# A token and channel mixer on one core: channel products in groups of six feature blocks, two places for token products in each chunk

## The chip, the cores and the metric

The kernel runs on one core of one Trainium2 chip. The metric is the time of one execution in microseconds (us). The engines are named as the profile names them: PE is TensorE (PEld its weight loads), DVE is VectorE, ACT is ScalarE, POOL is GpSimd, SP is SyncE, which here only issues transfers.

## What is computed

Of a batch of 8 sequences with 4096 tokens and 192 features, the kernel computes a softmax-weighted sum over seven earlier tokens (eight heads of 24 features), and feeds it to a mixer with two pairs of products. The mixer's four weight matrices are float64, and the kernel converts them.

```python
w = softmax(weight_gen, over the 7 taps)
x = sum over k of w[:, :, head, k] * x_pad[:, s + k]        # (8, 4096, 192)
h = relu(x.T @ w_tok1) @ w_tok2                             # tokens: 4096 -> 256 -> 4096
u = x + h.T
out = u + relu(u @ w_ch1) @ w_ch2                           # channels: 192 -> 1536 -> 192
```

Products keep nearly full float32 precision: each operand is split in a high and a low part, and a product is three matmuls (high by high, high by low, low by high).

## The kernel before

A sequence is cut into eight chunks of 512 tokens, 64 chunks in all; chunk g belongs to sequence g // 8. Five kinds of work meet on PE:

- **First token product** (T1, `token1`, L497, L499, for the first two sequences L514): one chunk of the weighted sums against `w_tok1`, accumulated over the eight chunks of a sequence in `h1s`. All eight must be there before the sequence's second token products can start (`make_h1`).
- **Second token product** (T2, `token2`, L531): 10 matmuls that give u of one chunk.
- **First channel product** (C1, `channel1`). The 1536 hidden features are 12 blocks of 128, taken as six pairs. The 192 input features are 128 plus 64: for the 128 (`a_hi`, `a_lo`) a pair takes 6 matmuls on all 128 rows of the array (L574); for the other 64 (`c_hi`, `c_lo`) the two blocks of a pair use the two halves of the rows at once, 6 matmuls in 3 steps of two (L579). Within a group of pairs all L574 come first, then all L579.
- **Second channel product** (C2, `channel2`, L595): 10 matmuls on 128 rows for each pair, accumulated in `acc`.
- In the first 120 us, the weighted sums and T1 of the first sequence, and conversions of weights.

Before the change a group is two pairs: 24 matmuls of C1, 20 of C2, three groups to a chunk, 192 groups in all. C2 of a group follows C1 of the next group, so PE alternates C1, C2, C1, C2; after a C2 there is a place for one token product, T1 or T2 (`pick`).

Results of C1, T1 and T2 land in PSUM, in three places of two banks (`ps_w`, taken in turn); `acc` has the other two banks. From a place of C1 (`ph`), ACT writes the high part of relu (L582) and DVE the low part (L583) into a tile `h`, of which there are four. T1 and T2 start from a value that ACT copies into their place first (L490, L525); T1 of a sequence's first chunk from zeros that DVE writes (`memset`, L487). After T2, ACT and DVE move u to the single tile `uf` (L538 to L543), and `u_parts` splits it into `a_hi`, `a_lo`, `c_hi`, `c_lo` (two tiles of each, L550 to L555). `acc` of a chunk is set from `uf` by ACT (`seed`, L603), after DVE has taken the chunk before out of it (`store`, L612, L613); ACT then moves the result to `out_tile` in 12 pieces (L622).

DVE's other large work is the weighted sums of later chunks (`attention`, L214, L228; POOL adds part of them by DMA, L232), up to twelve chunks ahead. Weights of `w_tok2` are converted from float64 chunk by chunk in the first 250 us (`convert`: three ACT steps L155 to L157, three DVE steps L159 to L161, then `split`, L166, L167), and those of `w_tok1` come back from DRAM for each later T1 (`load_w1`, `val<-s`, L379, or `w<-s`, L390).

The order on each engine is fixed when the program is built. A planner (`pump`) keeps a clock for each engine (`at`), with cost constants (`C1`, `C2`, `T1` and others), and fills ACT and DVE with pieces of the chains (`attentions`, `turns`, conversions, `store`, `u_parts`) up to a limit that depends on when the next `h` is due (`next_lo`, `SLACK`). On the chip each engine works through its list in order and waits where an operand or a place is not ready.

Of the kernel before, what the change touches and what calls it, by code (L numbers as in the profile page):

```python
# [21 lines left out]
def mixer_kernel(ctx: ExitStack, tc: tile.TileContext, x, wg, wt1, wt2, wc1, wc2, out):  # L22
# [13 lines left out]
    NQ = NP // 2  # L36
# [226 lines left out]
    def two_parts(m):  # L263
# [9 lines left out]
        if m // NCH >= F1:  # L273
            yield "a", 860, hi
            yield "v", 880, lo
# [205 lines left out]
    def token1(m):  # L481
# [4 lines left out]
        if i == 0:  # L486
            nc.vector.memset(th[:, :, cols], 0.0)  # L487
            h1s[b] = late.tile([P, KR, 2 * D], F32, tag="h1s", name="h1s")[:, :, cols]
        else:
            nc.scalar.copy(th[:, :, cols], h1s[b])  # L490
        yield
        if b >= F1:
            xh = xht.pop(m)
            for r in range(KR):
                for c in range(CT):
                    rs = slice(r * P, (r + 1) * P)
                    nc.tensor.matmul(th[:, r, 0:2 * D], w[:, c, 0, rs], xh[:, c, :], start=False, stop=False,  # L497
# [3 lines left out]
        else:  # L501
            token1_float(th, w, m, None, CT - 1)
# [16 lines left out]
    def token2(m, up=None):  # L519
# [25 lines left out]
    def u_parts(m):  # L545
# [3 lines left out]
        a_hi, a_lo, c_hi, c_lo = (late.tile([P, N], F32R, tag=x, name=x, bufs=2) for x in ("a_hi", "a_lo", "c_hi", "c_lo"))  # L549
# [15 lines left out]
    def channel1(g, q):  # L565

        a_hi, a_lo, c_hi, c_lo = ut[g]
        pairs = [2 * q, 2 * q + 1]
# [11 lines left out]
        for p in pairs:  # L580
            h = ht[g, p] = late.tile([P, 2, 2, N], F32R, tag="h", name="h", bufs=4)
# [5 lines left out]
    def channel2(g, q):  # L587
        acc = acc_t[g]
        for p in (2 * q, 2 * q + 1):
# [66 lines left out]
    LAST = 690  # L656
    T1, T1F, T2 = 2264, 2600, 2270
    TOP, LOW = 1000, 1180
    h_at, w_at, h1_at, h1s_at = {}, deque([0.0] * 3), {0: 0.0}, [0.0]
    free = {"acc": 0.0, "u": 0.0, "t": 0.0}  # L660
    pr_free = deque([0.0] * PR)
    xa_at, soft_at, wg_at, stored_at = {}, {}, {}, {}
# [40 lines left out]
    def pump(limit, keys=()):  # L703

        scalar = 0
        while True:
            best = None
            now = max(at["act"], at["pe"])
            end = max(at["pe"], w_at[0], w_at[1]) + C1 - LAST + LATE
# [34 lines left out]

    def next_lo():

        return max(at["act"], max(at["pe"], w_at[0], w_at[1]) + C1 - LAST + HOP) + TOP + HOP

# [5 lines left out]
             "done": NCH - 1, "w1": NCH}  # L754

    def raw_free(tag):

        if state["jobs"]:
            job, *what = state["jobs"].popleft()
            fetch_w2(*what, tag) if job is convert_w2 else fetch_channel(*what, tag)  # L760
            add_chain(job(*what), max(at["pe"], at["dve"]) + LOAD if at["pe"] > 0 else SOON, (job, *what))
# [47 lines left out]
    with tc.tile_pool(name="pro", bufs=1) as pro, \  # L809
# [30 lines left out]
        for m in range(NCH):  # L840
# [43 lines left out]
        state["jobs"] = deque((convert_w2, i) for i in range(1, NCH))  # L884
# [16 lines left out]
    load_xt(2)  # L901
    run(last)
    at["dve"], at["act"] = 3500, 1500
    chains[0:0] = [Chain(attentions()), Chain(turns()), Chain(soft)]
    add_chain(convert_channel("c2", 2), 0.0, ("c2", 2))
# [3 lines left out]
    def begin_token1():  # L909
        m, t = ready.popleft()  # L910
        it = token1(m)
        next(it)
        return it, m, on("act", 480 if m < F1 * NCH else 900, t, w_at.popleft(), h1s_at[0])

    def do_token1(it, m, t):
# [3 lines left out]
        pump(end + SLACK_M)  # L919
# [5 lines left out]
        while state["w1"] < min(m + 1 + (m + 1 >= F1 * NCH), NG - 1):  # L925
# [8 lines left out]
    def do_token2(it, m, t):  # L934
        next(it)
        t = on("pe", T2, t, h1_at[m // NCH])
        pump(t + SLACK_M)
        next(it, None)
        t = on("dve", 690, on("act", 1250, t))
# [8 lines left out]
    def token1_ready(soon=100):  # L948
        return ready and ready[0][0] in w1t and ready[0][1] <= at["pe"] + soon
# [5 lines left out]
    def pick(g, q, soon):  # L955
        final = (g + 1) % NCH == 0 and (g + 1) // NCH not in h1t and g + 1 < NG
        first = token1_ready(soon)
        if first and (final or q != 1 and ready[0][0] <= g + NCH + 2):
            return do_token1, begin_token1()
        if token2_ready(g + 1, soon):  # L960
            return do_token2, begin_token2(g + 1)
        if first and ready[0][0] <= g + NCH + 2:
            return do_token1, begin_token1()

    seed(0)
    for g in range(NG + 1):
        for q in range(NQ if g < NG else 1):
            if g == 0 and q > 0:
                need(lambda: ("w1a", 1) in done)
            if g == 1 and q == 0:  # L970
                need(lambda: ("c2", 2) in done, ("c2", 2))
            picked = None
            if g < NG:
                channel1(g, q)
                end = on("pe", C1, w_at.popleft(), w_at.popleft(), free["u"] if q == 0 else 0.0)
                for t in (end - LAST, end):
                    h_at[g, q] = on("dve", LOW, on("act", TOP, t))
                    w_at.append(h_at[g, q])
                picked = pick(g, q, C2)
            n = g * NQ + q - 1  # L980
            if n >= 0:
                prev = divmod(n, NQ)
                channel2(*prev)
# [11 lines left out]
            pump(next_lo() + (SLACK if g > NCH else SLACK0))  # L995
            if g == NG:
                break
            picked = picked or pick(g, q, 100)
            if picked is None:
                continue  # L1000
            picked[0](*picked[1])
            pump(next_lo() + SLACK)
        if state["token2"] < g + 1 < NG:
            while (g + 1) // NCH not in h1t:
                need(token1_ready, ("w1", state["token1"] + 1), ("x", state["token1"] + 1))
                do_token1(*begin_token1())
            need(lambda: g + 1 in w2t and g + 1 in xbt, (convert_w2, g + 1))
            do_token2(*begin_token2(g + 1))
        need(lambda: g + 1 in ut or g + 1 >= NG, ("u", g + 1))
# [29 lines left out]
```

## Time and profile before

| | before |
|---|---|
| median of 3 runs | 2193.71 us (2193.71 to 2195.42) |
| the profiled execution | 2193.25 us, its span 2191.5 us |
| PE busy | 98% of the span |
| DVE, ACT busy | 71%, 58% |

The span runs from the first to the last instruction; 1.8 us of the execution lie around it. Busy time of PE says little of its pace, since matmuls overlap: a matmul of 512 columns is shown 390 to 400 ns long, while one starts every 227 ns. So PE is read by the starts of its matmuls: the distance from one to the next is what the step costs.

### The profile page before, as it was taken

The numbers are of one execution on the slowest core, as the hardware profiler recorded it, in microseconds if no ns is written. First come the engines' busy times: TensorE is split into PE (matmuls) and PEld (weight loads), VectorE is DVE, ScalarE is ACT, GpSimd is POOL, SyncE is SP. The second block draws the span as 40 slices with busy tenths as digits, with TensorE's granted clock in tenths as the row PEclk, the third lists the DMA queues.
The fourth block names the chain that finished last, engine by engine and source line by source line (L and its number), as shares of the span: only waits on it lengthen the run. The fifth ranks groups of instructions, "written<-read, shape, count | busy, mean of one in ns | idle before, by whom it ended". The sixth has DMA issues, their size and how long they took to land.

```text
span 2191.5 us, 27185 instructions
## 1 busy us (share of the span) xinstructions
PE 2139.4 (98%) x10438; PEld 1671.6 (76%) x10438; DVE 1545.9 (71%) x1756; ACT 1264.6 (58%) x1972; POOL 164.8 (8%) x202
## 2 busy tenths in 40 slices
PE   7989999799999999999999999999999999999998
PEld 5757777677777877777777777777777777777776
DVE  8987887688888868777776876867787764333333
ACT  5557665456655655556565555556555565555554
POOL 0000111001110010000000010000100000000000
PEclk9999999899999999999999999999999999999999
DMA  7665778768778866755675665666667563222210
GB/s 274 216 222 156 196 203 192 205 179 241 206 209 248 225 178 174 195 139 175 174 200 167 182 164 153 189 170 189 176 176 195 139 169 96 68 68 68 64 34 18
DMA packets 165826, 366.66 MB, mean 167 GB/s; under 512 B 16456, under 2 KB 104264, under 8 KB 150336
## 3 DMA queue, kind: packets, MB, share of 16 engines
q1 hardware_dynamic: 138304, 285.74, 41.8%
q0 software_dynamic: 26496, 77.61, 18.3%
q8 instruction: 82, 1.34, 0.2%
q10 hardware_dynamic: 896, 1.57, 0.2%
q14 instruction: 48, 0.39, 0.1%
HBM read 225.13 MB, written 70.52 MB: 135 GB/s over the span
## 4 chain that ended last, share of the span: by engine, by line
PE 91%; DMA 3%; DVE 2%; ACT 2%; issue 1%; SPq 1%; POOL 0%; ACTq 0%; POOLq 0%; DVEq 0%
PE acc L595 39%; PE ph L574 23%; PE ph L579 13%; PE up L531 6%; PE tapsum L340 3%; PE th L497 3%; PE th L514 2%; PE th L499 2%; ACT out_tile L622 1%; DMA xb<-xs 1%; DMA xt<-in_x_dram 1%; PE turn L350 0%; DMA xs<-t 0%; ACT h L582 0%; DMA s<-w 0%
## 5 line engine op out<-in xcount | busy, mean ns | idle before, releaser
L595 PE MATMUL acc<-h,w2s 128*128 128x512 f32 x3840 | 926.3, 395 | 0.0
L595 PEld LDWEIGHTS acc<-h,w2s 128*128 128x128 f32 x3840 | 706.1, 188 | 208.2 <-issue 59.8
L583 DVE SCALAR_TENSOR_TENSOR h<-ph,h 128x1024 fp32r<-128x1024 f32 x384 | 451.7, 1218 | 328.9 <-ACT h L582 327.0
L582 ACT ACTIVATE h<-ph 128x1024 fp32r<-128x1024 f32 x384 | 373.2, 1025 | 366.0 <-PE ph L579 365.2
L214 DVE TENSOR_TENSOR pr<-xt,wn 128x768 f32<-128x768 f32 x336 | 312.0, 949 | 7.0 <-DMA xa<-pr 6.7
L574 PE MATMUL ph<-a_hi,w1a_hi 128*128 128x512 f32 x768 | 303.3, 395 | 9.3 <-ACT a_hi L550 7.4
L574 PE MATMUL ph<-a_lo,w1a_hi 128*128 128x512 f32 x768 | 301.0, 392 | 1.7 <-DVE a_lo L552 1.6
L574 PE MATMUL ph<-a_hi,w1a_lo 128*128 128x512 f32 x768 | 300.9, 392 | 0.0
L232 POOL DMA_DIRECT2D xa<-pr x176 | 151.2, 859 | 1447.4 <-DVE pr L228 1167.2
L603 ACT COPY acc<-uf 128x1024 f32<-128x1024 f32 x64 | 65.1, 1017 | 262.2 <-DVE oc L613 262.2
L622 ACT COPY out_tile<-oa 32x256 f32<-32x256 f32 x512 | 206.7, 404 | 6.8
L574 PEld LDWEIGHTS ph<-a_hi,w1a_hi 128*128 128x128 f32 x768 | 145.2, 189 | 39.6 <-ACT a_hi L550 8.9
L579 PE MATMUL ph<-c_hi,w1c_hi 64*128 64x512 f32 x768 | 171.6, 444 | 0.0
L574 PEld LDWEIGHTS ph<-a_lo,w1a_hi 128*128 128x128 f32 x768 | 145.2, 189 | 34.1 <-DVE a_lo L552 3.7
L574 PEld LDWEIGHTS ph<-a_hi,w1a_lo 128*128 128x128 f32 x768 | 145.4, 189 | 28.3
L531 PE MATMUL up<-w,h 128*128 128x512 f32 x630 | 156.8, 396 | 5.5 <-ACT up L525 5.4
L228 DVE TENSOR_TENSOR pr<-pr 128x768 f32<-128x768 f32 x160 | 152.7, 954 | 4.0
L579 PE MATMUL ph<-c_lo,w1c_hi 64*128 64x512 f32 x768 | 151.6, 391 | 0.0
L579 PE MATMUL ph<-c_hi,w1c_lo 64*128 64x512 f32 x768 | 150.8, 389 | 0.0
L531 PEld LDWEIGHTS up<-w,h 128*128 128x128 f32 x630 | 119.7, 191 | 32.5 <-ACT up L525 7.2
L579 PEld LDWEIGHTS ph<-c_hi,w1c_hi 64*128 64x128 f32 x768 | 71.7, 183 | 77.4 <-issue 66.5
L543 DVE TENSOR_TENSOR uf<-up,uf 64x512 f32<-64x512 f32 x63 | 42.9, 681 | 109.1 <-ACT uf L539 109.1
(83 smaller groups left out, 2054.1 us busy)
## 6 DMA issues: line engine op xcount, KB each, us to landing
w<-s SPq DMA_DIRECT2D x96, 1024.0 KB
xa<-pr POOLq DMA_DIRECT2D x176, 384.0 KB, 5.4
xt<-in_x_dram SPq DMA_DIRECT2D x56, 960.0 KB
out_dram<-out_tile SPq DMA_DIRECT2D x128, 192.0 KB
xs<-t SPq DMA_DIRECT2D x58, 384.0 KB
xb<-xs SPq DMA_DIRECT2D x348, 64.0 KB
raw<-in_moe_w_tok_dram SPq DMA_DIRECT2D x16, 1024.0 KB
s<-w POOLq DMA_DIRECT2D x8, 1024.0 KB, 6.9
```

Of the source, the lines that this page charges most:

```text
L214: nc.vector.tensor_mul(t.rearrange("p t (h g) -> p (t h) g", h=H).rearrange("p (o n) g -> p o n g", o=1), x_k, w)
L228: nc.vector.tensor_add(sums[m], sums[m], prt.pop(m))
L232: nc.gpsimd.dma_start(xat[m].rearrange("p t d -> p (t d)"), sums[m].rearrange("p t d -> p (t d)"), accum_op=ALU.add)
L340: nc.tensor.matmul(ps[:, n, 0:half * D], ident, prs[k][:, n * half:(n + 1) * half, :], start=k == 0, stop=k == K - 1)
L497: nc.tensor.matmul(th[:, r, 0:2 * D], w[:, c, 0, rs], xh[:, c, :], start=False, stop=False, skip_group_check=True)
L531: nc.tensor.matmul(up[:, n, :], h1[:, k, d], w[:, l, k * N:(k + 1) * N], start=k == 0 and j == 0 and not seeded, stop=k == KR - 1 and j == ...
L574: nc.tensor.matmul(ph[p][:, j, :], w[:, fs], u, start=n == 0, stop=False)
L579: nc.tensor.matmul(ph[p][:, j, :], w[rows, p * P:(p + 1) * P], u[rows], start=False, stop=n == 2)
L582: nc.scalar.activation(h[:, :, 0, :], ph[p], AF.Relu)
L583: nc.vector.scalar_tensor_tensor(h[:, :, 1, :], ph[p], 0.0, h[:, :, 0, :].bitcast(F32), op0=ALU.max, op1=ALU.subtract)
L595: nc.tensor.matmul(acc[:, n, :], w2s[:, f, d], h[:, j, l, :], start=False, stop=f == NF - 1 and i == len(steps) - 1, skip_group_check=True)
L622: nc.scalar.copy(dst, src[to:to + Q].rearrange("p (n e d) -> p n e d", n=2, d=Q)[:, n])
```

## The change

Six things change in the program. A group is three pairs (six feature blocks) instead of two, so there are two groups to a chunk, 128 in all, and a group takes all three PSUM places. `h` has five tiles; for that, `a_hi`, `a_lo`, `c_hi` and `c_lo` have one tile each, and `u_parts` of a chunk waits until the last C1 of the chunk before is done. At each of the two places of a chunk T2, T1 or both can stand (`picks`). T1 of a first chunk needs no zeros: its first matmul overwrites. The second chunk's `w_tok2` weights are fetched and converted before the last third of `w_ch2`. T1's weights are fetched two ahead from the fourteenth chunk on, and the planner's constants and limits are other ones.

```diff
-    NQ = NP // 2
+    PQ = 3
+    NQ = NP // PQ
@@ two_parts, load_w1
+            yield "w", 0, lambda: free["xh"]
...
+            w1_at[m] = at["pe"] + FETCH
@@ token1
-            nc.vector.memset(th[:, :, cols], 0.0)
...
-                    nc.tensor.matmul(th[:, r, 0:2 * D], w[:, c, 0, rs], xh[:, c, :], start=False, stop=False,
+                    nc.tensor.matmul(th[:, r, 0:2 * D], w[:, c, 0, rs], xh[:, c, :], start=i + c == 0, stop=False,
...
-            token1_float(th, w, m, None, CT - 1)
+            token1_float(th, w, m, 0 if i == 0 else None, CT - 1)
@@ token2
+            nc.scalar.copy(u[c, 1, :], up[e, 1, :])
             nc.scalar.copy(u[:, 0, :], up[:, 0, :])
-            nc.scalar.copy(u[c, 1, :], up[e, 1, :])
@@ u_parts
-        a_hi, a_lo, c_hi, c_lo = (late.tile([P, N], F32R, tag=x, name=x, bufs=2) for x in ("a_hi", "a_lo", "c_hi", "c_lo"))
+        a_hi, a_lo, c_hi, c_lo = (late.tile([P, N], F32R, tag=x, name=x) for x in ("a_hi", "a_lo", "c_hi", "c_lo"))
+        yield "gate", 0, lambda: state["channel1"] >= m * NQ
+        yield "w", 0, lambda: free["parts"]
@@ channel1, channel2
-        pairs = [2 * q, 2 * q + 1]
+        pairs = range(PQ * q, PQ * (q + 1))
...
-            h = ht[g, p] = late.tile([P, 2, 2, N], F32R, tag="h", name="h", bufs=4)
+            h = ht[g, p] = late.tile([P, 2, 2, N], F32R, tag="h", name="h", bufs=5)
...
-        for p in (2 * q, 2 * q + 1):
+        for p in range(PQ * q, PQ * (q + 1)):
@@ the planner's constants
+    FETCH = 6000
-    SOON = 500
-    SLACK = 900
-    SLACK0 = 1000
+    SOON = 5500
+    SLACK = 2500
-    LATE = 300
-    C1, C2 = 4390, 4540
+    LATE = 1500
+    C1, C2 = 6570, 6820
@@ the weights of the second chunk
-                fetch_channel("c2", 2)
+                fetch_w2(1)
...
-        state["jobs"] = deque((convert_w2, i) for i in range(1, NCH))
+        state["jobs"] = deque([(convert_channel, "c2", 2)] + [(convert_w2, i) for i in range(2, NCH)])
@@ do_token1
-        while state["w1"] < min(m + 1 + (m + 1 >= F1 * NCH), NG - 1):
+        while state["w1"] < min(m + 1 + (m >= F1 * NCH - 3), NG - 1):
@@ the token products of a place
-    def pick(g, q, soon):
...
+    def picks(g, soon):
+
+        two = token2_ready(g + 1, soon)
+        if two:
+            yield do_token2, begin_token2(g + 1)
+        if token1_ready(soon) and ready[0][0] <= g + NCH + (2 if not two else BEHIND):
+            yield do_token1, begin_token1()
```

Three places show how the order moves. The first is PE in the ninth chunk, the second half of one C1 (after its L574), the C2 behind it; `ph` and `h` carry the numbers of their tiles. Before:

```order
L579 MATMUL ph_3307<-c_hi_2942,w1c_hi_77 128x512 x2
L579 MATMUL ph_3307<-c_hi_2942,w1c_lo_78 128x512 x2
L579 MATMUL ph_3307<-c_lo_2943,w1c_hi_77 128x512 x2
L579 MATMUL ph_3308<-c_hi_2942,w1c_hi_77 128x512 x2
L579 MATMUL ph_3308<-c_hi_2942,w1c_lo_78 128x512 x2
L579 MATMUL ph_3308<-c_lo_2943,w1c_hi_77 128x512 x2
L595 MATMUL acc_3159<-h_3229,w2s_79 128x512 x10
L595 MATMUL acc_3159<-h_3232,w2s_79 128x512 x10
```

The same place with the change:

```order
L583 MATMUL ph_3281<-c_hi_2961,w1c_hi_77 128x512 x2
L583 MATMUL ph_3281<-c_hi_2961,w1c_lo_78 128x512 x2
L583 MATMUL ph_3281<-c_lo_2962,w1c_hi_77 128x512 x2
L583 MATMUL ph_3282<-c_hi_2961,w1c_hi_77 128x512 x2
L583 MATMUL ph_3282<-c_hi_2961,w1c_lo_78 128x512 x2
L583 MATMUL ph_3282<-c_lo_2962,w1c_hi_77 128x512 x2
L583 MATMUL ph_3283<-c_hi_2961,w1c_hi_77 128x512 x2
L583 MATMUL ph_3283<-c_hi_2961,w1c_lo_78 128x512 x2
L583 MATMUL ph_3283<-c_lo_2962,w1c_hi_77 128x512 x2
L599 MATMUL acc_3204<-h_3149,w2s_79 128x512 x10
L599 MATMUL acc_3204<-h_3152,w2s_79 128x512 x10
L599 MATMUL acc_3204<-h_3155,w2s_79 128x512 x10
```

A run of steps on half the rows now holds nine steps instead of six, and a run on all rows 30 matmuls of C2 instead of 20: 64 fewer changes from the one to the other and back.

The second is ACT right after the first chunk's `c_lo`, where the channel products begin. Before (`w_828` is the second chunk's `w_tok2`):

```order
L166 CAST w1a_hi<-val 128x768
L603 COPY acc<-uf 128x1024
L582 ACTIVATE h<-ph 128x2x512 x2
L155 ACTIVATE val<-raw 128x1024
L156 ACTIVATE val<-val,below 128x1024
L182 ACTIVATE wg<-wg 128x448
L582 ACTIVATE h<-ph 128x2x512 x2
L157 ACTIVATE val<-val 128x1024
L155 ACTIVATE val<-raw 128x768
L582 ACTIVATE h<-ph 128x2x512 x2
L166 CAST w_828<-val 128x1024
```

With the change (`w_777` is the second chunk's `w_tok2`):

```order
L156 ACTIVATE val<-raw 128x1024
L157 ACTIVATE val<-val,below 128x1024
L158 ACTIVATE val<-val 128x1024
L167 CAST w1a_hi<-val 128x768
L607 COPY acc<-uf 128x1024
L586 ACTIVATE h<-ph 128x2x512 x3
L156 ACTIVATE val<-raw 128x768
L157 ACTIVATE val<-val,below 128x768
L183 ACTIVATE wg<-wg 128x448
L158 ACTIVATE val<-val 128x768
L586 ACTIVATE h<-ph 128x2x512 x3
L167 CAST w_777<-val 128x1024
```

The three conversion steps of the second chunk (128x1024) now stand ahead of `w1a_hi`, `acc` and the first relu; T2 of the second chunk follows the first C2 instead of the second.

The third is SP's queue towards the end of the second sequence's T1 (`val<-s` are T1's weights, `xs<-t` a transposed chunk that DVE writes). Before:

```order
L94 DMA xt<-in_x_dram 128x1920
L111 DMA wg<-in_weight_gen_dram 128x224 x2
L299 DMA xs_2773<-t 128x768
L379 DMA val<-s_84 128x1024 x3
L299 DMA xs_2821<-t 128x768
```

With the change:

```order
L301 DMA xs_2418<-t 128x768
L381 DMA val<-s_84 128x1024 x2
L98 DMA xt<-in_x_dram 128x768
L99 DMA xt<-in_x_dram 1x768
L103 DMA xt<-in_x_dram 112x1152
L103 DMA xt<-in_x_dram 14x1152
L95 DMA xt<-in_x_dram 128x1920
L112 DMA wg<-in_weight_gen_dram 128x224 x2
L637 DMA out_dram<-out_tile 32x8x192 x2
L301 DMA xs_2758<-t 128x768
L381 DMA val<-s_84 128x1024 x2
```

The weights of the sequence's last T1, the first of the three `val` before, are the second of the earlier two now, ahead of a chunk's loads, an output and the transpose `xs_2758`.

## Rows read from the trace of the kernel before

**Rows 1.** The page: engines (busy us, share, instructions), and PE's clock in tenths.
```profile
PE 2139.4 (98%) x10438; PEld 1671.6 (76%) x10438; DVE 1545.9 (71%) x1756; ACT 1264.6 (58%) x1972; POOL 164.8 (8%) x202
...
PEclk9999999899999999999999999999999999999999
```

**Rows 2.** Timeline of PE, one group in mid-kernel: start us, shown length, engine, line, operation.
```profile
702.97 0.39 PE L574 MATMUL ph<-a_hi,w1a_hi 128*128 128x512 f32 x1
...
705.46 0.39 PE L574 MATMUL ph<-a_lo,w1a_hi 128*128 128x512 f32 x1
705.78 0.50 PE L579 MATMUL ph<-c_hi,w1c_hi 64*128 64x512 f32 x2
706.12 0.40 PE L579 MATMUL ph<-c_hi,w1c_lo 64*128 64x512 f32 x2
...
707.04 0.40 PE L579 MATMUL ph<-c_lo,w1c_hi 64*128 64x512 f32 x2
707.37 4.83 PE L595 MATMUL acc<-h,w2s 128*128 128x512 f32 x20
712.04 0.33 PE L497 MATMUL th<-xh,w 128*128 128x384 f32 x1
...
714.29 0.41 PE L574 MATMUL ph<-a_hi,w1a_hi 128*128 128x512 f32 x1
```

**Rows 3.** Groups by line: busy us, mean ns of one, idle before, releaser.
```profile
L583 DVE SCALAR_TENSOR_TENSOR h<-ph,h 128x1024 fp32r<-128x1024 f32 x384 | 451.7, 1218 | 328.9 <-ACT h L582 327.0
L582 ACT ACTIVATE h<-ph 128x1024 fp32r<-128x1024 f32 x384 | 373.2, 1025 | 366.0 <-PE ph L579 365.2
...
L525 ACT COPY up<-xb 128x1024 f32<-128x1024 f32 x63 | 64.5, 1023 | 0.8
...
L543 DVE TENSOR_TENSOR uf<-up,uf 64x512 f32<-64x512 f32 x63 | 42.9, 681 | 109.1 <-ACT uf L539 109.1
...
L538 ACT COPY uf<-up 128x512 f32<-128x512 f32 x63 | 37.0, 587 | 71.0 <-PE up L531 70.5
```

**Rows 4.** Timeline of PE, 122 to 205 us, where the channel products begin; idle before in brackets.
```profile
124.44 0.50 PE L574 MATMUL ph<-a_hi,w1a_hi 128*128 128x512 f32 x1
...
133.44 0.63 PE L574 MATMUL ph<-a_hi,w1a_hi 128*128 128x512 f32 x1 [1.83 <-DVE h L583]
...
160.45 0.80 PE L574 MATMUL ph<-a_hi,w1a_hi 128*128 128x512 f32 x1 [5.50 <-ACT a_hi L550]
...
183.90 4.04 PE L531 MATMUL up<-w,h 128*128 128x512 f32 x10 [2.75 <-ACT up L525]
...
202.33 4.82 PE L595 MATMUL acc<-h,w2s 128*128 128x512 f32 x20
```

**Rows 5.** Timeline of PE, 388 to 419 us, the second sequence's last T1.
```profile
388.57 2.76 PE L514 MATMUL th<-xa,val 128*128 128x192 f32 x16
399.30 4.82 PE L514 MATMUL th<-xa,val 128*128 128x192 f32 x16 [7.96 <-DMA val<-s]
406.20 4.15 PE L531 MATMUL up<-w,h 128*128 128x512 f32 x10 [2.09 <-ACT up L525]
...
418.67 3.70 PE L595 MATMUL acc<-h,w2s 128*128 128x512 f32 x15
```

**Rows 6.** Timeline of SP's queue in the same stretch.
```profile
394.68 1.41 SPq L379 DMA_DIRECT2D val<-s  x3
```

**Rows 7.** Windows: us, PE, PEld, DVE, ACT, POOL busy (count), granted clock, DMA share, GB/s.
```profile
145.00:165.00 20.00, 13.92 (x56) 9.60 (x55) 16.34 (x21) 14.17 (x18) 1.43 (x2) 0.83 0.68 217
...
388.00:404.00 16.00, 8.04 (x36) 7.47 (x34) 9.09 (x11) 0.96 (x2) 1.72 (x2) 0.79 0.89 262
...
600.00:800.00 200.00, 200.00 (x1006) 158.91 (x1003) 170.57 (x203) 121.18 (x191) 22.95 (x27) 1.00 0.80 218
```

**Rows 8.** Timeline of DVE at one sequence's first T1.
```profile
884.17 0.70 DVE L487 MEMSET th<- 128x768 f32 x1 [0.16 <-DVE h L583]
```

**Rows 9.** Timeline of PE at the same T1.
```profile
885.12 0.41 PE L497 MATMUL th<-xh,w 128*128 128x384 f32 x1 [0.59 <-DMA xb<-xs]
```

More of the change, by code (lines that the diff above doesn't have):

```diff
@@ L659, in mixer_kernel @@
     h_at, w_at, h1_at, h1s_at = {}, deque([0.0] * 3), {0: 0.0}, [0.0]
-    free = {"acc": 0.0, "u": 0.0, "t": 0.0}
+    free = {"acc": 0.0, "u": 0.0, "t": 0.0, "parts": 0.0, "xh": 0.0}
     pr_free = deque([0.0] * PR)
-    xa_at, soft_at, wg_at, stored_at = {}, {}, {}, {}
+    w1_at, xa_at, soft_at, wg_at, stored_at = {}, {}, {}, {}, {}
     ready = deque()
@@ L753, in mixer_kernel @@
              "summed": NCH - 1, "turned": FT - 1, "parts": NCH - 1, "kept": FT - 1, "stored": -1, "out": -1,
-             "done": NCH - 1, "w1": NCH}
+             "done": NCH - 1, "w1": NCH, "channel1": 0}
     def raw_free(tag):
@@ L918, in do_token1 @@
         state["token1"] = m
-        pump(end + SLACK_M)
+        free["xh"] = end
+        pump(end + SLACK_M, (), end + SLACK_A)
         next(it, None)
@@ L948, in token1_ready @@
     def token1_ready(soon=100):
-        return ready and ready[0][0] in w1t and ready[0][1] <= at["pe"] + soon
+        return ready and ready[0][0] in w1t and max(ready[0][1], w1_at.get(ready[0][0], 0.0)) <= at["pe"] + soon
     def token2_ready(m, soon=100):
@@ L969, in mixer_kernel @@
                 need(lambda: ("w1a", 1) in done)
-            if g == 1 and q == 0:
-                need(lambda: ("c2", 2) in done, ("c2", 2))
-            picked = None
+            picked = []
             if g < NG:
                 channel1(g, q)
[L975 to L979, printed above, removed]
+                state["channel1"] += 1
+                end = on("pe", C1, *(w_at.popleft() - i * FIRST for i in range(PQ)), free["u"] if q == 0 else 0.0)
+                for i in range(PQ):
+                    w_at.append(on("dve", LOW, on("act", TOP, end - (PQ - 1 - i) * LAST)))
+                h_at[g, q] = w_at[-1]
+                free["parts"] = end
+                picked = list(picks(g, C2))
             n = g * NQ + q - 1
@@ L982, in mixer_kernel @@
                 prev = divmod(n, NQ)
+                if n == 1:
+                    need(lambda: ("c2", 2) in done, (convert_channel, "c2", 2))
                 channel2(*prev)
@@ L994, in mixer_kernel @@
                     free["acc"] = on("act", 1050, free["acc"])
-            pump(next_lo() + (SLACK if g > NCH else SLACK0))
             if g == NG:
                 break
[L998 to L1001, printed above, removed]
-            pump(next_lo() + SLACK)
[L1003 to L1009, printed above, removed]
+            if not picked:
+                if 0 < g < NCH - 1 and q == 0:
+                    need(lambda: g + 1 in w2t, (convert_w2, g + 1))
+                picked = list(picks(g, 2000))
+            if not picked:
+                pump(next_lo() + SLACK)
+                picked = list(picks(g, 100))
+            for do, it in picked:
+                do(*it)
+            if q < NQ - 1:
+                pump(next_lo() + SLACK)
+        if g + 1 < NG:
+            if state["token2"] < g + 1:
+                while (g + 1) // NCH not in h1t:
+                    need(token1_ready, ("w1", state["token1"] + 1), ("x", state["token1"] + 1))
+                    do_token1(*begin_token1())
+                need(lambda: g + 1 in w2t and g + 1 in xbt, (convert_w2, g + 1))
+                do_token2(*begin_token2(g + 1))
+            need(lambda: g + 1 in ut, ("u", g + 1))
+            pump(next_lo() + SLACK)
     run(*[chain([c.item], c.items) for c in chains if c.item is not None])
```

31 lines of the change are left out of this document (15 added, 16 removed).

## The prediction

> **What bounds the kernel now.** I read the page first: PE is busy 98% of the span, DVE 71%, ACT 58% [rows 1]. Since busy PE says little of its pace, I went to the distances between matmul starts in PE's timeline, then to PE's waits, and last to the windows with the granted clock. From some 420 us on PE hardly waits at all: between 600 and 800 us it is busy in all 200 of 200 us at a granted clock of 1.00, with DVE at 85% and ACT at 61% [rows 7]. There the time is the sum of PE's own steps, and only a cheaper step shortens it. Before that, PE loses time in two stretches: where the channel products begin (waits of 1.83, 5.50 and 2.75 us [rows 4]) and at the end of the second sequence's T1 (7.96 and 2.09 us [rows 5]). Both also show the clock at its lower level for a part: 0.83 granted on the mean of 145 to 165 us, 0.79 of 388 to 404 us, where 0.5 would be 1.2 GHz throughout and 1.00 is 2.4 GHz [rows 7].
>
> **Part 1: fewer changes between full and half rows.** In a steady group 11 steps on all rows take 705.46 - 702.97 = 2.49 us, 0.2265 us each. The step into the half rows takes 0.32 us, the first step there 0.34, while the next four take 0.23 each (706.12 to 707.04), and the way out takes 0.33. C2 takes 712.04 - 707.37 = 4.67 us, 0.14 more than 20 steps of 0.2265 [rows 2]. So a group pays about 0.09 + 0.11 + 0.10 + 0.14 = 0.44 us beside its matmuls; the whole group, 712.04 - 702.97 = 9.07 us less 32 x 0.2265 and 6 x 0.233, gives 0.42. I take 0.42. None of it recurs at the second pair inside the group, where the steps go on at 0.23, so it belongs to the group and not to the pair. 192 groups become 128: 64 x 0.42 = 26.9 us less (0.40 to 0.44 give 25.6 to 28.2). In steady state a group becomes 18 x 0.2265 + 9 x 0.232 + 0.3 = 6.46 us of C1 and 30 x 0.2265 + 0.14 = 6.94 us of C2. All of this lies on PE, so all of it counts, as long as no new wait takes it.
>
> **Part 2: what could wait now in steady state.** The three places of PSUM are all taken by a group's C1, so the token product behind the next C2 goes into the first place of the group just done, and the group after that needs the token product's place third. I set the end of a C1 as zero. Its first pair is complete some 1.2 us before, so ACT (1.025 us a tile) and DVE (1.218 us) [rows 3] empty the first place by about 1.1, the second by 2.4. The third relu waits for a tile: the group's third `h` takes the fifth tile in turn, which is the first of the group before, read by C2 until 10 x 0.2265 + 0.2 = 2.5. So it ends at 3.5 on ACT and 4.8 on DVE. Queued behind it on ACT is the copy into the token product's place (1.023 us [rows 3]), done by 4.6; PE wants it when C2 ends, at 6.9. Spare: 2.3 us. T2 then ends at 9.2, and its place is wanted 12 x 0.2265 = 2.7 us later, by the third pair; the copy of 0.587 us on ACT and, behind it, 0.681 us on DVE [rows 3] empty it in about 1.5 us. Spare: 1.2 us, one DVE operation. `u_parts`, with one tile each now, can begin only at the end of the chunk's last C1, queued on ACT behind the relu at 3.5; `a_lo` comes at 5.5, and the next chunk's third matmul wants it at 7.4, later where a T1 stands between. Spare: 1.9 us. DVE's forced idle time (1.2 us at the third relu, some 2 us before the transposes) fits beside its 171 us of work in 200 [rows 7]. I count nothing for the steady part, and 0 to 10 us, of which I take 3, for the first sequences, where some chunks have no T1 between and DVE carries the conversions too.
>
> **Part 3: the end of the second sequence's T1.** From 388.57 to 418.67 us PE does two T1 (2.5 us each), one T2 (2.27) and one C1 (4.40) [rows 2, 5]: 11.7 us of work in 30.1, so 18.4 are lost. 7.96 are the wait for the last T1's weights, issued by SP only at 394.68 [rows 6], behind a transpose that DVE finished late. The change issues them a chunk earlier, so this wait goes. What is late next is the chain of the same three products: the last T1's start from `h1s` (about 1.4 us, two copies on ACT after the T1 before), T2 after it (2.09 stays), C1 after T2 (1.9). That is 5.4 us of waits, and the clock will still fall for some of it: before, the loss beyond the waits was 18.4 - 7.96 - 2.09 - 1.9 = 6.5 us. I keep 2 of it (0 to 4). New loss 7.4, gain 11 us (9 to 13).
>
> **Part 4: no zeros.** The memset that ends at 884.87 lets PE start the sequence's first T1 only at 885.12, 0.75 us late [rows 8, 9]; PE's timeline has five such places of 0.65 to 0.76 us. Without the memset T1 needs only the place, which DVE left 0.7 us earlier. Gain 3.7 us (0 to 3.7).
>
> **Part 5: where the channel products begin.** From 124.44 to 202.33 us stand seven C1, five C2 and two T2: 58.7 us of work in 77.9, so 19.2 are lost [rows 2, 4]. With the change the second group cannot start before the first is emptied: relu of the first pair now stands behind three conversion steps, `w1a_hi` and the copy into `acc`, so PE waits about 2.7 us where it waited 1.83. T2 of the second chunk then comes some 5 us earlier on PE and its weights are ready for it within about 1 us; but DVE has seven pieces of the last third of `w_ch2` and of the sums ahead of `uf`, so C1 of the second chunk waits about 5.4 us, as it did (5.50). T2 of the third chunk stands behind `acc` on ACT: about 4.9 us against 2.75. The waits add up to about 15 us against 11.7, with the slow clock beside them as before. I take a loss of 2 us more (4 less to 8 more).
>
> **Sum**, against the profiled execution of 2193.25 us (span 2191.5 and 1.8 around it; the median of the runs is 2193.71): 2193.25 - 26.9 - 11 - 3.7 + 2 + 3 = 2156.7 us. The prologue up to 120 us and the end (transposes, moves and output after the last C2) keep their order and are counted at nothing.
>
> **Rivals.**
> *DVE falls behind in the first two sequences.* Work on DVE to the end of the second sequence is the same, in a stretch that is shorter by about 5 us plus the waits that go. For it: DVE is at 85% as late as 600 to 800 us, and it now waits for the third relu in each group. Against it: those waits vanish when DVE is late. Price: 10 to 25 us, PE waiting for `a_lo` or for an emptied place in 10 to 16 chunks by 1 to 1.5 us. About 2167 to 2182, say 2174.
> *The cost belongs to pairs, not to groups.* Then part 1 gives nothing, and 2193.25 - 11 - 3.7 + 5 = 2183.5 is left. Against it: the steps of the second pair go on at 0.23 [rows 2].
> *A bubble in every chunk, ending slower.* The place of a token product is wanted 2.7 us after its end and emptied in 1.5 if ACT and DVE are free. One tile of DVE's relu in front (1.218 us) just fits; two make 1.5 + 2.4 - 2.7 = 1.2 us of wait, in 64 chunks 77 us: 2234 us. It is slower than before from 36.6 / 64 = 0.57 us in each chunk on. For it: no place is spare any more. Against it: DVE is held in step just before by the transposes, which wait for C2, and stands idle when T2 ends. The Trainium skill, "Perfetto Trace Analysis", section Optimization Strategy, names this case: the same gap repeating on the engine that should be full can mean that PSUM has no room for the next tile. This trace, with one place of three always spare beside C1, shows no such gap; the change takes that place away.
>
> **How the numbers follow.** Forecast (2147 to 2166) 0.60. DVE behind 0.20. Cost by pairs 0.05. Bubble, slower 0.07; the same bubble small enough to end within 0.2% of before 0.03. Below 2147, by a start without slow clock, 0.05. The range leaves out the bubble, the lowest case and the upper end of the others: 2147 to 2181. A measurement of this kernel can tell about 0.2% from no change, here 4.4 us. Faster: 0.60 + 0.20 + 0.05 + 0.05 = 0.90; same 0.03; slower 0.07.
>
> **What would show it.** Part 1: in the changed kernel's timeline of PE a steady C1 start to C1 start of 13.4 us, 15.67 with a token product, and a granted clock of 1.00. Part 2: waits of PE on L586, L587 or L545 near zero after 450 us; a repeated wait at the thirteenth matmul of a C1 is the bubble. Part 3: two T1 next to each other near 380 us with under 2 us between. Part 4: no wait at a sequence's first T1. Part 5: about 21 us lost between 124 and 196 us. If the distances in a steady group are 13.6 instead of 13.4, part 1 is wrong; if they hold and the time does not fall, a wait is back.

## The result and the profile after

The changed kernel takes 2167.57 us (median of 4 runs, 2166.28 to 2170.26) against 2194.04 us: 0.988 of the time, with a 95% interval of 0.9863 to 0.9897. The profiled execution took 2166.28 us, its span 2164.5. The forecast was 2157 us within 2147 to 2181; the time is in the range. The sum was made for the profiled execution, which is 9.6 us above it.

The page of the changed kernel, engines and PE's clock, as in [rows 1]:

```profile
PE 2110.9 (98%) x10438; PEld 1678.7 (78%) x10438; DVE 1542.7 (71%) x1749; ACT 1274.6 (59%) x1972; POOL 166.5 (8%) x202
...
PEclk9999999999999999999999999999999999999999
```

The shares say as little as before. The steps are read from PE's timeline, here a group with a T1 behind it (columns as in [rows 2]):

```profile
806.44 0.39 PE L578 MATMUL ph<-a_hi,w1a_hi 128*128 128x512 f32 x1
...
810.34 0.40 PE L578 MATMUL ph<-a_lo,w1a_hi 128*128 128x512 f32 x1
810.66 0.50 PE L583 MATMUL ph<-c_hi,w1c_hi 64*128 64x512 f32 x2
...
812.93 7.12 PE L599 MATMUL acc<-h,w2s 128*128 128x512 f32 x30
819.89 0.33 PE L499 MATMUL th<-xh,w 128*128 128x384 f32 x1
...
822.14 0.41 PE L578 MATMUL ph<-a_hi,w1a_hi 128*128 128x512 f32 x1
```

From C1 to C1 with a T1 it is 822.14 - 806.44 = 15.70 us; 15.67 was predicted. Where nothing waits, C1 takes 6.457 us (6.493 behind a T1) and C2 6.937, 13.39 for a group where 13.4 was predicted: 26.8 us a chunk where two pairs took 27.2. Next PE's waits (line, releaser: us in total, times, longest), and windows (columns as in [rows 7]; the last one is of the kernel before):

```profile
PE up L533 <- ACT up L527: 10.4, 4, 4.5
PE ph L578 <- DVE uf L545: 7.7, 8, 1.7
PE ph L578 <- ACT a_hi L554: 3.9, 2, 2.0
PE ph L578 <- DVE h L587: 2.5, 1, 2.5
PE ph L578 <- ACT h1s L506: 2.3, 1, 2.3
```

```profile
145.00:165.00 20.00, 15.30 (x58) 10.93 (x56) 18.07 (x23) 12.27 (x16) 1.44 (x2) 0.74 0.62 201
...
410.00:760.00 350.00, 343.00 (x1720) 274.46 (x1719) 284.98 (x336) 212.00 (x333) 33.75 (x39) 1.00 0.74 205
760.00:1500.00 740.00, 740.00 (x3727) 595.47 (x3725) 558.62 (x656) 441.34 (x694) 64.84 (x75) 1.00 0.66 180
```

```profile
410.00:760.00 350.00, 347.59 (x1729) 274.73 (x1729) 292.22 (x343) 216.61 (x340) 35.09 (x41) 0.99 0.77 216
```

From 760 us on PE is full, 740 of 740. Between 410 and 760 us it is idle for 7.0 us, where it was idle for 2.4 in the same window before (1.9 of them still behind the second sequence's T1). The second wait of the list, for `uf`, makes up 6 of the 7: PE waits for the place that T2 had, until T2's results have been moved to `uf`. In seven of the eight cases it stands at the thirteenth matmul of a C1, the third pair's first; one of these:

```profile
644.36 0.70 DVE L616 STREAM_TRANSPOSE oa<-acc 128x512 f32<-128x512 f32 x1
...
648.69 0.50 PE L578 MATMUL ph<-a_hi,w1a_hi 128*128 128x512 f32 x1 [0.86 <-DVE uf L545]
```

The eighth is at the seventh matmul: a T1 follows T2 there and takes the next place, so that the second pair needs T2's. It is the case in which DVE is latest, and it shows the whole chain, all engines in order of time (C2 has ended at 607.1):

```profile
607.12 2.43 PE L533 MATMUL up<-w,h 128*128 128x512 f32 x10
607.75 0.95 DVE L215 TENSOR_TENSOR pr<-xt,wn 128x768 f32<-128x768 f32 x1
608.73 0.96 DVE L229 TENSOR_TENSOR pr<-pr 128x768 f32<-128x768 f32 x1
...
609.61 0.95 DVE L215 TENSOR_TENSOR pr<-xt,wn 128x768 f32<-128x768 f32 x1
...
610.47 0.71 DVE L616 STREAM_TRANSPOSE oa<-acc 128x512 f32<-128x512 f32 x1
...
611.11 0.67 DVE L617 STREAM_TRANSPOSE oc<-acc 128x512 f32<-128x512 f32 x1
...
611.81 1.02 ACT L607 COPY acc<-uf 128x1024 f32<-128x1024 f32 x1 [4.28 <-DVE oc L617]
...
612.86 0.58 ACT L540 COPY uf<-up 64x512 f32<-64x512 f32 x1
...
613.46 0.59 ACT L541 COPY uf<-up 128x512 f32<-128x512 f32 x1
...
614.08 0.68 DVE L545 TENSOR_TENSOR uf<-up,uf 64x512 f32<-64x512 f32 x1 [1.57 <-ACT uf L541]
...
614.81 0.50 PE L578 MATMUL ph<-a_hi,w1a_hi 128*128 128x512 f32 x1 [1.62 <-DVE uf L545]
```

`acc` could be read from 607.1 on, but DVE has three pieces of the weighted sums in its list first and begins the transposes at 610.47, 3.4 us late. `seed` (L607) waits for both, T2's copies stand behind `seed` (it reads `uf`, which they overwrite), and DVE's last step stands behind both copies: 614.81 - 610.47 = 4.34 us from the first transpose to an empty place, and 648.69 - 644.36 = 4.33 in the case above. So T2's results, complete at 609.4, leave PSUM only from 612.86 on.

### The profile page after: what moved, and what is told of

Its sections match the earlier page's. It is cut to its first block, busy times and chain, and to the rows that moved or that the text cites. A ratio compares the mean times of both kernels' runs of the same rounds, so it can differ in the third digit from the quotient of the medians.

```text
span 2164.5 us, 27209 instructions
## 1 busy us (share of the span) xinstructions
PE 2110.9 (98%) x10438; PEld 1678.7 (78%) x10438; DVE 1542.7 (71%) x1749; ACT 1274.6 (59%) x1972; POOL 166.5 (8%) x202
## 3 DMA queue, kind: packets, MB, share of 16 engines
q0 software_dynamic: 26496, 77.61, 18.7%
## 4 chain that ended last, share of the span: by engine, by line
PE 86%; DVE 6%; DMA 3%; ACT 3%; issue 1%; POOL 0%; SPq 0%; ACTq 0%; DVEq 0%; POOLq 0%
PE acc L599 36%; PE ph L578 21%; PE ph L583 12%; PE up L533 6%; PE tapsum L342 3%; PE th L499 3%; PE th L501 1%; PE th L516 1%; DVE pr L215 1%; DVE h L587 1%; DMA xa<-pr 1%; DMA xs<-t 1%; DMA xt<-in_x_dram 1%; ACT h L586 1%; DVE pr L229 1%
## 5 line engine op out<-in xcount | busy, mean ns | idle before, releaser
L599 PE MATMUL acc<-h,w2s 128*128 128x512 f32 x3840 | 908.5, 393 | 0.0
L586 ACT ACTIVATE h<-ph 128x1024 fp32r<-128x1024 f32 x384 | 379.9, 1025 | 389.9 <-PE ph L583 225.4
L607 ACT COPY acc<-uf 128x1024 f32<-128x1024 f32 x64 | 65.1, 1018 | 246.0 <-DVE oc L617 246.0
L533 PE MATMUL up<-w,h 128*128 128x512 f32 x630 | 157.2, 397 | 10.4 <-ACT up L527 10.4
L583 PE MATMUL ph<-c_hi,w1c_hi 64*128 64x512 f32 x768 | 165.1, 427 | 0.0
```

What stands on the lines that cost most here:

```text
L533: nc.tensor.matmul(up[:, n, :], h1[:, k, d], w[:, l, k * N:(k + 1) * N], start=k == 0 and j == 0 and not seeded, stop=k == KR - 1 and j == ...
L583: nc.tensor.matmul(ph[p][:, j, :], w[rows, p * P:(p + 1) * P], u[rows], start=False, stop=n == 2)
L586: nc.scalar.activation(h[:, :, 0, :], ph[p], AF.Relu)
L599: nc.tensor.matmul(acc[:, n, :], w2s[:, f, d], h[:, j, l, :], start=False, stop=f == NF - 1 and i == len(steps) - 1, skip_group_check=True)
L607: nc.scalar.copy(acc_t[g], uft.pop(g))
```

## The experiments

Times are medians, and the difference is to the changed kernel's 2167.57 us; each was run beside the kernel before, whose medians lay between 2192.76 and 2193.81. Differences under 4 us can't be told by the times alone; there the waits are compared.

### What a change of rows costs

C1 of the changed kernel written pair by pair, so that a group goes to half rows and back three times:

```diff
         for p in pairs:
             for j in range(2):
...
-        for p in pairs:
             for n, (w, u) in enumerate(((w1c_hi, c_hi), (w1c_lo, c_hi), (w1c_hi, c_lo))):
```

> The changed kernel with C1 written pair by pair: six steps on all rows, three double steps on half rows, three times in a group; the same matmuls in another order, so 2 more changes of rows and back in each of 128 groups. Theory (a change costs 0.42 us wherever it stands): +256 x 0.42 = +107 us, 2275 us; a steady C1 of 7.3 us instead of 6.46. Rival (the 0.42 us belongs to the hand-over between C1 and C2 and their PSUM places, not to the rows): C1 stays at 6.5 us and the time at 2168 within 4 us.

2261.12 us, 93.6 more; 1.0314 of before (1.0298 to 1.033). One C1 in its timeline of PE:

```profile
1108.63 0.41 PE L578 MATMUL ph<-a_hi,w1a_hi 128*128 128x512 f32 x1
...
1110.12 0.50 PE L582 MATMUL ph<-c_hi,w1c_hi 64*128 64x512 f32 x2
...
1111.02 0.50 PE L578 MATMUL ph<-a_hi,w1a_hi 128*128 128x512 f32 x1
...
1115.97 7.09 PE L598 MATMUL acc<-h,w2s 128*128 128x512 f32 x30
```

From C1 to C2 it is 1115.97 - 1108.63 = 7.34 us, behind a T1. A steady C1 takes 7.302 us instead of 6.457: 0.845 for two more changes, 0.42 each, the price read from the trace of before. 128 x 0.845 = 108 us; some 15 of them came back, of which 10 are waits of PE that got shorter: none for `uf` is left in its list. The hand-over between C1 and C2 is the same here, and a change without it costs as much; so the rival, that the hand-over is what costs, falls.

### Groups of two pairs again

```diff
-    PQ = 3
+    PQ = 2
...
-    C1, C2 = 6570, 6820
+    C1, C2 = 4390, 4540
...
-                if n == 1:
+                if n == 2:
```

> The changed kernel with groups of two pairs again (192 groups), all else as changed. Theory (each full-to-half-to-full change of rows costs PE about 0.42 us, once in a group): the distance of a steady C1 and C2 goes back from 13.41 us for three pairs to 9.07 us for two, 27.2 us a chunk against 26.8, so +26 us; the waits that came with the third pair's place (some 12 us, of PE on uf, h1s and up) go, since a place is spare again, so 2167.6 + 26 - 12 = 2182 us (2178 to 2194). Rival (the cost is of pairs, and the changed kernel won by something else): distance 8.94 us, time within 5 us of 2168.

2201.64 us, 34 more, above the range that was expected; 1.0038 of before (1.0024 to 1.0051). Its C1 takes 4.402 us and its C2 4.665 again, so the steps alone make 192 x 9.067 - 128 x 13.394 = 26.4 us, as the theory has it. The rest are waits that had not been expected, in its list:

```profile
PE ph L578 <- DVE a_lo L556: 15.3, 18, 1.8
...
PE ph L578 <- DVE h L587: 8.5, 3, 5.3
```

With one tile each, `a_hi` to `c_lo` can be filled only after the chunk's last C1; the prediction had counted 1.9 us to spare for that behind a C2 of three pairs, and one of two pairs, 4.67 us, is 2.27 shorter. So the single tiles, which made room for the fifth `h`, go with groups of three pairs; a run with two pairs and two tiles of each was not made. (In one of the 64 chunks, chunk 4, this run leaves x out for 320 of 512 tokens. Its T2, at 244.0 us, stood in the place that the second sequence's first T1, without zeros, had used at 218.7, with only another T1, at 230.6, between: the first T1's first matmul overwrites 192 of a bank's 512 columns, and in the others T2's matmuls overwrote the value copied there instead of adding to it. With three pairs the next user of the place is a C1, which overwrites all 512, each of the seven times. The work and its time are the same.)

### Fewer pieces in front of the transposes

```diff
-                pump(at["pe"] + SLACK_M)
+                pump(at["pe"] + SLACK_M - 1600)
```

> The changed kernel with one planner limit lowered: pieces of other work are put in front of the two transposes of acc on DVE only if they are due to end 1.2 us before C2 does, not up to 0.4 us behind it. Theory (PE waits for the third place because DVE comes late to the transposes, seed waits for them, and T2's copies for seed): PE's waits at the thirteenth matmul of a C1 for uf (7.7 us in 8 places) fall under 2.5 us, time 2162 us (2160 to 2165). Rival (DVE is late because it has waited for the DMA out of the single tile t): the waits stay over 5 us and the time within 2 us of 2167.6. Second rival (the pieces put off are missed elsewhere): slower, 2170 or more.

2184.76 us, 17 more; 0.9966 of before. Its waits of PE:

```profile
PE up L533 <- ACT up L527: 16.1, 5, 7.0
PE ph L578 <- ACT a_hi L554: 16.1, 8, 2.3
...
PE ph L578 <- DVE uf L545: 1.9, 2, 0.9
```

With the pieces away the waits for `uf` fall from 7.7 to 1.9 us. But this run doesn't show the cause by itself, since the weighted sums come later and the planner falls into another order: T1 stands directly behind T2 21 times instead of 7, which leaves more time to empty T2's place in PSUM, and the first chunk of each later sequence gets its T2 directly ahead of its own C1, which then waits some 2 us for `a_hi`.

So that the order of the products stays, the same edit with more room for the pieces elsewhere:

```diff
-    SLACK = 2500
+    SLACK = 3300
...
-                pump(at["pe"] + SLACK_M)
+                pump(at["pe"] + SLACK_M - 1600)
```

> The limit in front of the two transposes lowered by 1.6 us as in the run before with that edit, and SLACK raised from 2500 to 3300, so that DVE's pieces that may not stand there stand at the other places; the order of T1, T2, C1 and C2 on PE then stays that of the changed kernel but for one chunk (in the run before it had changed throughout). Theory (filler pieces in front of the transposes make seed, and so the emptying of T2's place, late): PE's waits for uf fall from 7.7 us to under 2, no wait for a_hi at the start of a sequence, 2161 to 2164 us. Rival (DVE has more work than room in the first 750 us, and what is moved is missed at the next place): other waits of PE (on h, a_lo, up) grow by as much, 2167 or more.

2173.1 us, 5.5 more; 0.9901 of before (0.9886 to 0.9916). T1 stands directly behind T2 seven times, as in the changed kernel, and no wait for `uf` is left: so the pieces in front of the transposes caused these waits. But PE waits 18.8 us for `up` instead of 10.4. One of these places, DVE first, then ACT:

```profile
659.49 0.98 DVE L295 STREAM_TRANSPOSE t<-xa 128x768 f32<-128x768 f32 x1 [6.72 <-DMA xs<-t]
...
669.86 2.35 DVE L587 SCALAR_TENSOR_TENSOR h<-ph,h 128x1024 fp32r<-128x1024 f32 x2
```

```profile
671.11 1.02 ACT L527 COPY up<-xb 128x1024 f32<-128x1024 f32 x1 [6.68 <-DVE h L587]
```

DVE stands 6.72 us before a transpose into `t`, whose last content is still on its way to DRAM, and then works through all pieces in its list before it comes to `h`; the place for T2 comes free too late by 4.28 us. The wait has moved to the next thing that DVE is late for. That is the rival, and the kernel is no faster for it.

### DVE's waits for the transfer out of t

```diff
-    KEEP = 6000
+    KEEP = 12000
```

> The changed kernel with one planner constant raised: the tile t counts as in use for 12 us after its DMA is issued instead of 6, so the next transpose into t is placed later. Theory of the filler pieces in front of the transposes: the waits of DVE for that DMA (61.5 us in 19 places) fall under 20 us, but PE's waits for uf stay over 5 us, time 2166 to 2169 us. Rival (DVE comes late because of these waits): PE's waits for uf fall under 2.5 us and the time to 2161 to 2164 us.

2169.27 us, 0.9891 of before (0.9878 to 0.9905). DVE's waits for this transfer, in the changed kernel

```profile
DVE t L295 <- DMA xs<-t: 61.5, 19, 6.3
```

are gone from its list, and PE's for `uf` are as before:

```profile
PE ph L578 <- DVE uf L545: 7.8, 9, 1.7
```

So these 61 us of DVE are not why the transposes come late.

### The chain behind seed

Three ways to make the 4.3 us shorter. First DVE's last step written between the two copies, then also `seed` as two copies:

```diff
             nc.scalar.copy(u[c, 1, :], up[e, 1, :])
-            nc.scalar.copy(u[:, 0, :], up[:, 0, :])
...
         nc.vector.tensor_add(u[c, 1, :], up[c, 1, :], u[c, 1, :])
+        if seeded:
+            nc.scalar.copy(u[:, 0, :], up[:, 0, :])
```

> The changed kernel with DVE's last step of u (64x512, 0.68 us) written between ACT's two copies of u instead of behind both; nothing else. Theory (T2's place is emptied too late because seed comes late and the three steps behind it run one after the other): DVE runs beside the second copy, the place comes free 0.53 us sooner, and PE's eight waits for uf (7.7 us) shrink by that each to about 3.6 us: 2163.5 us (2162 to 2165). Rival (the wait is DVE's backlog and only moves to another reader): waits of PE in sum as before, time within 1.5 us of 2167.6.

```diff
-        nc.scalar.copy(acc_t[g], uft.pop(g))
+        u = uft.pop(g)
+        for n in range(2):
+            nc.scalar.copy(acc_t[g][:, n, :], u[:, n, :])
```

> The same, and seed written as two copies of one bank each, so that the first needs only the first transpose of acc: it runs beside the second transpose, and seed ends 0.46 us sooner. Theory: PE's waits for uf fall to about 1.4 us, 2161 us (2160 to 2163). Rival (seed is not in the chain; DVE's own lateness is all of it): no better than the kernel with the first edit alone, or 0.15 us a chunk worse where ACT is short.

2171.65 us (0.9899 of before, 0.9886 to 0.9913) and 2175.69 us (0.9919, 0.9907 to 0.9932): neither helps. In the first, at the chain shown above, ACT's second copy now waits for DVE's step, as DVE's step had waited for the copy:

```profile
613.32 0.71 DVE L617 STREAM_TRANSPOSE oa<-acc 128x512 f32<-128x512 f32 x1
...
616.32 0.68 DVE L544 TENSOR_TENSOR uf<-up,uf 64x512 f32<-64x512 f32 x1 [0.97 <-ACT uf L540]
...
617.04 0.58 ACT L546 COPY uf<-up 128x512 f32<-128x512 f32 x1 [0.75 <-DVE uf L544]
...
617.68 0.50 PE L579 MATMUL ph<-a_hi,w1a_hi 128*128 128x512 f32 x1 [1.42 <-ACT uf L546]
```

617.68 - 613.32 = 4.36 us, no less. The theory of the edit fell: writing the steps in this other order doesn't let them overlap. So `uf` and `acc` were given a tile for each half:

```diff
-        acc_t[g] = ps_acc.tile([P, 2, 512], F32, tag="acc", name="acc")
-        nc.scalar.copy(acc_t[g], uft.pop(g))
+        acc_t[g] = acc_tiles()
+        for a, u in zip(acc_t[g], uft.pop(g)):
+            nc.scalar.copy(a, u)
...
-    uf_.append(late.tile([P, 2, N], F32, name="uf"))
+    uf_ += [late.tile([P, N], F32, name=x) for x in ("ua", "uc")]
...
+    def acc_tiles():
+        return [ps_acc.tile([P, 512], F32, tag=x, name=x) for x in ("acc0", "acc1")]
```

> The changed kernel with uf as two tiles and acc as two tiles of one bank each, seed as two copies; the planner's numbers are untouched. In the two runs on the order of these steps ACT's second copy waited for DVE's add, and the first seed copy for both transposes, though they touch different halves: the order is kept by tile. Theory: with a tile for each half the steps overlap, from the start of the transposes to an empty place 3.3 us instead of 4.3, PE's waits for uf fall from 7.7 us to about 1.5: 2161 us (2160 to 2164). Rival (the serial chain isn't what decides, DVE's lateness is): waits over 5 us, 2166 to 2169 us.

2164.61 us, 0.9864 of before (0.985 to 0.9879), the lowest of all, though 3 us are too little to tell from the changed kernel. The chain at the same place:

```profile
611.82 0.71 DVE L618 STREAM_TRANSPOSE oa<-acc 128x512 f32<-128x512 f32 x1
612.46 0.68 DVE L619 STREAM_TRANSPOSE oc<-acc 128x512 f32<-128x512 f32 x1
612.57 0.59 ACT L609 COPY acc<-ua 128x512 f32<-128x512 f32 x1 [3.68 <-DVE oa L618]
...
615.74 0.50 PE L579 MATMUL ph<-a_hi,w1a_hi 128*128 128x512 f32 x1 [1.25 <-DVE uc L546]
```

`seed` now begins beside the second transpose, and the place is empty after 3.92 us instead of 4.34; PE's waits for `uf` fall from 7.7 to 4.4 us in 7 places; 1.5 had been expected, and over 5 by the rival, so the run decides between them only in part. DVE's last step still begins only behind the second copy.

A further run has these tiles together with the two limits that kept the order of the products (`SLACK` 3300, and 1600 ns less room ahead of the transposes): 2159 to 2162 us were expected, and 2166 or more by the rival that DVE is short of time. It took 2168.58 us, 0.9887 of before (0.987 to 0.9903): no wait for `uf` is left, and PE waits 18.7 us for `up`, as with the limits alone (18.8). So the rival held again.

The last run puts DVE's step between the copies with the two tiles too (`ua` is not touched by it any more):

```diff
             nc.scalar.copy(uc[c], up1[e])
-            nc.scalar.copy(ua, up0)
...
         nc.vector.tensor_add(uc[c], up1[c], uc[c])
+        if seeded:
+            nc.scalar.copy(ua, up0)
```

> uf and acc as two tiles each, as in the run before with that edit, and DVE's last step of u written between ACT's two copies, so that it waits for the first copy alone (with two tiles and the old order it still waited for both). Theory (the serial chain behind seed sets when T2's place is empty): 0.5 us less in each of the seven waits that were left, 4.4 us in sum, to 1.5 or less; 2161 to 2163 us, the fastest. Rival (DVE is short of time before 750 us, and what one wait gives the next takes): waits for uf fall but those for up, h1s and a_hi grow, 2164 to 2167 us.

2167.07 us, 0.988 of before (0.9864 to 0.9897). The second copy waits for DVE's step again, and the chain takes 3.93 us; PE waits 5.7 us for T2's place in sum, and 6.5 instead of 3.9 for `a_hi`. ACT's copies and DVE's step, which take T2's results out of PSUM, come one after the other in each form that was tried. What they still share is the PSUM tile they read; whether that is the reason was not tried.

### The end of the second sequence's T1, and the zeros

```diff
-        while state["w1"] < min(m + 1 + (m >= F1 * NCH - 3), NG - 1):
+        while state["w1"] < min(m + 1 + (m + 1 >= F1 * NCH), NG - 1):
```

> The changed kernel with the one condition on T1's weights as before the change: fetched one ahead until the last T1 of the second sequence. Theory of part 3 of the prediction: the wait for the weights comes back between the two T1 near 388 us, 6 to 9 us, and the sum of PE's waits there goes from 5 back to 11 or more: 2174 to 2177 us. Rival (the weights are not late any more, since the transpose that held SP's queue now comes at another time): within 2 us of 2167.6.

2169.82 us, 0.9889 of before (0.9874 to 0.9904). The wait is back, but with 2.00 us instead of 7.96 [rows 5]:

```profile
393.24 4.52 PE L516 MATMUL th<-xa,val 128*128 128x192 f32 x16 [2.00 <-DMA val<-s]
```

SP issues the transfer at 388.38 us here, 6.3 us earlier than before [rows 6], since the transpose that stood ahead of it ends on DVE at 380.72 and not at 394.23; what holds the queue until 387.4 is now an output transfer. From the first of the two T1 to T2 PE needs 11.4 us instead of 8.9. By the medians, 2.25 us apart, the run can't be told from the changed kernel.

```diff
+            nc.vector.memset(th[:, :, cols], 0.0)
             h1s[b] = late.tile([P, KR, 2 * D], F32, tag="h1s", name="h1s")[:, :, cols]
...
-                    nc.tensor.matmul(th[:, r, 0:2 * D], w[:, c, 0, rs], xh[:, c, :], start=i + c == 0, stop=False,
+                    nc.tensor.matmul(th[:, r, 0:2 * D], w[:, c, 0, rs], xh[:, c, :], start=False, stop=False,
...
-            token1_float(th, w, m, 0 if i == 0 else None, CT - 1)
+            token1_float(th, w, m, None, CT - 1)
```

> The changed kernel with T1's zeros back in the place of a sequence's first T1 (DVE memset of 128x768, or 128x384 in the second sequence), and its first matmul adding to them. Theory of part 4: PE waits 0.65 to 0.76 us in five places again, +3.7 us, 2171 us. Rival (a place is filled so long before PE wants it that the zeros cost nothing): within 1 us of 2167.6. With three pairs the memset comes behind three relu steps of DVE instead of two, so more than 3.7 us, up to 1.2 us a sequence, 8 us, is possible too.

2169.42 us, 0.9888 of before (0.9874 to 0.9901). DVE writes the zeros seven times, and PE waits for them once, in the second sequence:

```profile
228.19 4.19 PE L517 MATMUL th<-xa,val 128*128 128x192 f32 x14 [2.62 <-issue]
```

In this place the zeros cost 2 us net: from the C2 in front, which ends at 225.4, to the end of the next C1 it takes 13.6 us, and 11.6 in the changed kernel, whose C1 waits 2.3 us for `h1s` there. In the six later sequences PE doesn't wait: the zeros are written 1.1 us or more before T1 begins. The rival holds there; the medians, 1.85 us apart, decide nothing.

## Why the prediction was right, and where it was off

**Part 1 held.** The group pays 6.457 + 6.937 - 48 x 0.2265 - 9 x 0.233 = 0.42 us beside its matmuls, as before; 64 fewer give 26.4 us by the steps (26.9 predicted). The experiment with more changes gives the same 0.42.

**Part 2 is the term that was mis-sized: about 15 us instead of 3.** Eleven C1s and one T2 between 209 and 750 us come through 0.5 to 2.7 us late each, 15 us in sum; 11.5 of it stand as idle time of PE in the rows, and the rest is in the shown length of the matmul before each gap and the slower start behind it. About 10 of the 15 are the waits for T2's place; the latest single C1, by 2.7 us, waits for a T1's place (`h1s`), which was not followed up. The step that failed is the sentence on T2's place: it counted the copies from T2's end, "1.5 us" against 2.7, with 1.2 us to spare. They stand behind `seed`, and `seed` behind two transposes, so 4.3 us count from the moment DVE begins the transposes, and the place is wanted 5.0 us after C2 ends (T2's 2.27 and 2.7) where no T1 follows T2. The spare is 0.7 us, and one piece of DVE's work (0.95) uses it up. The second half of the mistake was the reason against the bubble: "DVE is held in step just before by the transposes, which wait for C2". That is so after 760 us, where DVE is busy 559 of 740 us (75%); from 410 to 760 us, at 285 of 350 (81%), it comes to them up to 3.4 us late.

**The rivals.** DVE does fall behind early, much as that rival said: 15 us in 12 places, where it had 10 to 25 us in 10 to 16 chunks, and the time is at the lower end worked out for it, 2167. The bubble at the thirteenth matmul is there too, but in 7 chunks (and once at the seventh matmul) and not in 64. That the same gap repeating can mean that PSUM has no room for the next tile is what the Trainium skill, "Perfetto Trace Analysis", Optimization Strategy, says; this trace agrees, with eight gaps of 0.3 to 1.7 us, as long as DVE is late. Cost by pairs is refuted. The median lies 1.6 us above the band to which the forecast gave 0.60 (2147 to 2166); it is in the range because that was drawn to take in a part of the rivals.

**Part 3 held in size, only partly in its reason.** From the one T1 to the C1 behind T2:

```profile
387.55 2.76 PE L516 MATMUL th<-xa,val 128*128 128x192 f32 x16
391.45 2.87 PE L516 MATMUL th<-xa,val 128*128 128x192 f32 x16 [1.14 <-ACT th L492]
396.41 2.59 PE L533 MATMUL up<-w,h 128*128 128x512 f32 x10 [2.09 <-ACT up L527]
400.97 0.51 PE L578 MATMUL ph<-a_hi,w1a_hi 128*128 128x512 f32 x1 [1.97 <-ACT a_hi L554]
```

5.2 us of waits (5.4 predicted), and with the slow clock a loss of about 8.2 where 7.4 was predicted: a gain of 10 (11). But the earlier fetch gives only some 2 to 4 of it (2.5 us up to T2, and 1.9 behind it, in the run without it). The rest is there without it, in the other order of the products and of SP's queue; which part of that order does it was not run apart.

**Part 4 held by its waits; its reason is not shown.** No T1 at a sequence's start waits, 3.7 us less. But in the new order zeros would cost PE something only once. In the old order they ended 0.25 us before T1 began [rows 8, 9]; that they were the cause there is read from this alone, the row itself names a transfer of `xb`, which T1 doesn't read, and no run of the old order without them was made.

**Part 5** came out 2 us better: from 123.84 to 194.04 us stand four C1, three C2 and two T2, 51.2 us of work in 70.2, so 19.0 us are lost instead of 21. The C1 of the second chunk waits 1.97 us, not 5.4; the low clock (0.74 in 145 to 165 us, 0.83 before) took part of that back. Which of the edits at the start did it was not tried apart.

Against the sum: +12 (part 2), +0.5 (part 1), +0.7 (part 3) and -2.2 (part 5) make 11.0 where 9.6 are to be explained. Of the other -1.4, 0.6 lie in the prologue, which was counted at nothing: the channel products begin at 123.84 us and not at 124.44 [rows 4]. The rest was not followed up.

## What to carry over

When a change takes away a spare buffer, follow its emptying back through each engine's list to the last thing that must wait, here from a copy over `seed` to two transposes, and count the spare from there; a count from the producer's end assumes that the readers stand ready. An engine that works through a list in order, as DVE here at 81%, is late where pieces that could wait stand in front of an urgent one; moving them here only moved the wait. A cost of switching can be priced by an experiment that adds more of it: here it needed no other change and gave 0.42 us again.

## What the runs showed of the hardware

The clock fell behind short waits: PE waited 1.14 us, did a T1, waited 2.09, did a T2, waited 1.97 and began a C1, in which its matmuls stand 0.43 us apart from 402.6 to 405.5 us. The granted clock of that window is 0.50, the lower level, 1.2 GHz (columns as in [rows 7]); from 396 to 401 us it was 1.00, and after 405.6 us the matmuls stand 0.23 us apart again:

```profile
402.60:405.50 2.90, 2.90 (x8) 2.30 (x7) 2.90 (x4) 1.45 (x2) 0.85 (x1) 0.50 1.12 291
```

And a matmul that overwrites a part of a PSUM bank has a say in what a later accumulation does to the rest of the bank: in the run with two pairs the 320 columns of the place in chunk 4 that T1 had not written lost the value that ACT had copied there. The Trainium skill, "PSUM — Partial Sum Buffer", section The four PSUM rules, states it: such a first matmul clears the marks of the whole bank, a later one overwrites where the mark is clear, and a copy by ACT doesn't set it. The run agrees. So the removal of the zeros leans on the order that three pairs give, in which a C1 over the whole bank follows in the place of each sequence's first T1.
